# The last 800 steps of a fused attention and MLP kernel in another order, with other engines for some of them

## The chip, the cores and the metric
The kernel runs on one core of one Trainium2 chip. The metric is the device time of one execution in microseconds (us): 209.87 is the median of three runs before (209.62 to 209.92). A profiled run is an execution of its own. Engines are named as in the profile: PE is TensorE's matmuls, PEld its weight loads, DVE is VectorE, ACT is ScalarE, POOL is GpSimd, SP is SyncE, which issues DMAs.

## The reference
Attention over a window of 128 keys and the first 4 keys (sinks), for 4 batches, 8 heads, 768 positions and a head size of 64; its output is the input of an MLP with squared relu, 3072 tokens, 512 to 2048 to 512.

```python
rel = pos[:, None] - pos[None, :]
keep = is_sink | ((rel >= 0) & (rel < window))          # n_sink 4, window 128
scores = np.where(keep, scale * np.matmul(q, k.transpose(0, 1, 3, 2)), -1e9)
a = np.exp(scores - scores.max(-1, keepdims=True))
attn = np.matmul(a / (a.sum(-1, keepdims=True) + 1e-9), v)
x = attn.transpose(0, 2, 1, 3).reshape(B * S, H * D)    # 3072 x 512
r = np.maximum(x @ w_in, 0.0)
out = (r * r) @ w_out
```

## The kernel before
The work is cut into 992 steps, each a small function that issues one or a few instructions. A table, `ORDER`, lists the steps by number in the order in which they are issued. A letter behind a number names the engine of a step that can run on more than one (d DVE, a ACT, g POOL, p PE); without a letter it is the first engine that the step allows. A "+0" or "+1" names the pool of PSUM banks that it takes. `Plan.run` goes through the table from first to last. Every engine works through its own instructions in that order and waits at each for what it needs, so the table sets the queue of each engine, of SP's and POOL's DMA issues too, and the reuse of buffers, which are handed out as they come free in table order: eight `expm` buffers, three `r`, two `osb`, four `sg`, two times two pools of PSUM banks.

The stages of a batch, with the names that the profile shows and the lines that matter here:

- Loads. For batches 2 and 3, q, k and v are loaded by POOL's queue (`qn`, L402, and `v`, L414) and q and k are turned by SP's DMA transposes (`qkT`, L460). For batches 0 and 1 PE turns them (`pt`, L503).
- Scores: PE writes `ps` (L609) and the sinks' scores `pk` (L568); ACT takes exponentials into `expm` (L630) and `es` (L576).
- Masks: the steps `domask` set what lies outside the window to zero. A step with "g" issues two affine selects on POOL (L218), each on 128x512 values; a step with "d" multiplies by a triangle on DVE (L642), 128x1024 values at once. The first of a batch multiplies by `mask0` on DVE (L639).
- Values: PE writes `po` (L678), DVE takes reciprocals (L694) and scales (L695, `xn_sb`); the result is turned into `xT` by PE and a copy (`px`, L727, L192/L194) or by SP's DMA transposes (L709).
- Layer 1 of the MLP: batch 0 as plain products (L762, relu L776 or L778, squares L785 or L787). The other batches use a scheme of seven products for each block of 2x2 (L892) on sums of the inputs (`xs`, L854; `xd` is a spread copy) and of the weights (`wi`, L811). Partial results are kept by a copy `t` (ACT L192 or DVE L194), added and bounded by DVE (`r`, L942), put through a relu (L967 on ACT, L969 on DVE) and squared into `gT_sb` (L915 on ACT, L917 on DVE).
- Layer 2: mostly the same scheme (products `py`, L1239), on four sums of `gT_sb` that DVE makes from 16-bit values (`sg` and in place, L1213, 128x1024 each). Quarters of the output are copied (L192 on ACT, L194 on DVE) or added (L1253, DVE) into `osb`, and SP's queue stores them (L1282). The last tile ends in smaller pieces (L1100 and following).

A copy is issued at L192 when ACT makes it and at L194 when DVE makes it, whatever it copies; the tile's name tells which it is.

Of the kernel before, what the change touches and what calls it, by code (L numbers as in the profile page):

```python
# [21 lines left out]
990 1 0 2 7 8 9 10 11 12 13 14 15 16 17 18 56d 60a 55d 991+0 3 19 57+0 61d 20 5 6 4 62+1 65 59a 67+0 58a 21 64d 89d  # L22
63a 68+0 75+1 88d 69 70 76+1 22 71+0 77 23 72 73 78 24 94a 79+1 90+0 93d 92a 95+1 80 91d 81 96a 74 100+0 82 101+0 25
26 102 83+1 97d 66 84d 27 104 85 110+1 111+0 103g 86d 152+1 112 28 113d 105d 98+0 99 153 106+0 108 114 115d 154a 116+1
118 29 160+1 109 161 162a 107 30 119 117 120+0 31 155d 163a 122 121d 123d 32 168+0 156+1 331 33 172+0 157 169 164+1
170a 165 34 35 158d 173 166a 124+1 125a 127+0 36 159d 176+1 129a 177 126d 174a 140+1 133+1 37 128d 171d 142 136 180+1
181 282+0 38 178d 167d 137d 132+0 141+1 182a 130+0 39 283 40 144 143d 41 134 42 43 332 284 285 131 145d 146+0 175a 147
135g 278 179a 286 138+1 139 287 288 148+0 150 334 151d 44 149a 279 183d 289 184+1 290 185 193+0 280 281 200+0 201 291
194 45 204+1 196+0 202 46 203 205 198a 186 197 207a 293 206 187+0 199a 216+0+0 47 48 195a 217 49 188d 234+1+0 50 235
190+0 219 208+0 87 292 237 209 295 191 218 297+0 189 220 51 336 52 212 53 210a 294 211 255+0 252+1 254 299 298 256 54  # L30
253a 257 444 223+0+1 333 238d 445 192a 226 304 213 224 221+0 312 222 300 241+1+0 301 214+0 296 244 215 302 225 446
303d 242 306 260+0+0 236 462 263 307 314 337 316+0 245d 243d 315 227 308 313 447 318 319 464 246+0 261 247 239+0 448
240 320 321 228+0 475 322d 317 229 258+0 335 259 325 449 450 310 326 230+0 451 231 452 232 248+0 233 249a 327 250 251a
323 309 305 343+1 359+1 339 338 344 467 340 345 341 360 463 329 311 453 324 328 346 465 347 361 362 363 267+1+1 348
349 350 364 268 342 365d 270 351d 366 367 375+0 352 376 377 354 368 454 355 468 356d 370 369a 357 455 391+0 456 379
264 457 262 466 458 265+0 271 393 353 459 378 269 371 392 395 358a 266 372 272+0 373 381 380 382 474 374a 397 394 273
274+0 383d 276 277 396 275a 384 469 407 386 485+0+0 388d 718 472 387 470 460 486 398 410 461 408 389 412+1 488 471
478+1+0 409 399 473 385 479 400 487 330 413 688 402 414 428+0 404 401 403 405 430 416 429 418 432 406a 489 530+0 481
415 390 417 431 419 532 689 526 411 490+0 434 420 433 435 528 421 423 491 436 437 707 482 527 422a 533 424 480 534 690
708 476+0 477 425 439 440 441 691 535 442 531 483+1 426 529 484 443a 536 494+0+0 537 438a 497 692 427 495 568+0 545  # L40
539 540 570 564 566 492 693 694 695 542 498d 501+0+0 502 565 696 541 493 571 504 697 706 538 572 698 543 569 709
517+0+1 518 546 699 573 544 547 520 700 575 503d 510+0+0 701 574 549+0 496d 583 711 576 567 577 584 578 521d 513 505
# [1367 lines left out]
```

## Time and profile before

| | before |
|---|---|
| median of 3 runs | 209.87 us |
| the profiled execution | 209.26 us |
| its span | 207.6 us |
| PE busy | 199.6 us (96%) |
| DVE busy | 174.7 us (84%) |
| ACT busy | 133.9 us (64%) |
| POOL busy | 96.2 us (46%) |

The span runs from the first to the last recorded instruction; 1.66 us of the execution lie around it. Busy times of the engines overlap and don't add up to the span. Times of single rows are in microseconds from the start of the span; a bracket behind a row shows the idle time of the engine before it and who ended it. An instruction on DVE or ACT is shown until its result is written, and the next of the same engine starts a little earlier, so rows of one engine overlap by about 0.1 us.

### The profile page before, as it was taken

The numbers are of one execution on the slowest core, as the hardware profiler recorded it, in microseconds if no ns is written. First come the engines' busy times: TensorE is split into PE (matmuls) and PEld (weight loads), VectorE is DVE, ScalarE is ACT, GpSimd is POOL, SyncE is SP. The second block draws the span as 40 slices with busy tenths as digits, with TensorE's granted clock in tenths as the row PEclk, the third lists the DMA queues.
The fourth block names the chain that finished last, engine by engine and source line by source line (L and its number), as shares of the span: only waits on it lengthen the run. The fifth ranks groups of instructions, "written<-read, shape, count | busy, mean of one in ns | idle before, by whom it ended". The sixth has DMA issues, their size and how long they took to land.

```text
span 207.6 us, 6021 instructions
## 1 busy us (share of the span) xinstructions
PE 199.6 (96%) x2500; PEld 176.2 (85%) x2502; DVE 174.7 (84%) x342; ACT 133.9 (64%) x208; POOL 96.2 (46%) x137
## 2 busy tenths in 40 slices
PE   7969999999899999999999999999999999999993
PEld 7458997579878899889878988998889999999893
DVE  4387657498899998999998778999989998998853
ACT  2769458729998168898888458989871452584010
POOL 7799275699499927999333529000280000000000
PEclk9999999999999999999999999999999999999999
DMA  5999999999999999999999996901023220200205
GB/s 157 220 218 200 186 185 212 180 156 175 159 75 126 147 129 225 117 182 155 123 142 235 103 135 194 115 3 25 12 42 129 53 94 10 104 0 0 104 0 202
DMA packets 96042, 26.10 MB, mean 126 GB/s; under 512 B 86800, under 2 KB 93456, under 8 KB 96016
## 3 DMA queue, kind: packets, MB, share of 16 engines
q0 software_dynamic: 69248, 12.59, 86.5%
q1 hardware_dynamic: 25568, 12.49, 27.2%
q10 hardware_dynamic: 1200, 0.66, 1.1%
q8 instruction: 19, 0.31, 0.6%
q14 instruction: 7, 0.06, 0.1%
HBM read 27.30 MB, written 6.29 MB: 162 GB/s over the span
## 4 chain that ended last, share of the span: by engine, by line
PE 80%; DVE 6%; ACT 6%; DMA 4%; issue 2%; POOL 0%; ACTq 0%; POOLq 0%; DVEq 0%
PE py L1239 28%; PE pm L892 25%; PE pm L762 9%; PE po L678 6%; PE ps L609 4%; DMA v<-in_v_dram 4%; PE py L990 3%; ACT expm L630 2%; PE py L1100 2%; PE pt L503 1%; DVE r L942 1%; ACT gT_sb L915 1%; PE px L727 1%; DVE xn_sb L695 1%; ACT qkT L192 1%
## 5 line engine op out<-in xcount | busy, mean ns | idle before, releaser
L630 ACT ACTIVATE expm<-ps 128x1024 bf16<-128x1024 f32 (+1 forms) x48 | 43.8, 951 | 9.6 <-PE ps L609 7.6
L218 POOL TENSOR_SCALAR_AFFINE_SELECT expm<-expm 128x512 bf16<-128x512 bf16 x34 | 24.0, 740 | 42.2 <-DVE xn_sb L695 19.5
L942 DVE CUSTOM_DVE_ANT_0 r<-pm,t 128x512 bf16<-128x512 f32 x54 | 36.0, 684 | 1.6 <-PE pm L892 1.2
L1239 PEld LDWEIGHTS <-gT_sb 128*128 128x128 bf16 x320 | 30.4, 98 | 4.4 <-issue 0.6
L892 PEld LDWEIGHTS <-w_in_sb 128*128 128x128 bf16 x384 | 32.4, 114 | 1.7 <-issue 1.5
L192 ACT ACTIVATE t<-pm 128x512 f32<-128x512 f32 x42 | 24.7, 600 | 13.4 <-PE pm L892 12.7
L892 PEld LDWEIGHTS <-wi 128*128 128x128 bf16 x288 | 24.7, 114 | 0.8 <-issue 0.7
L1239 PEld LDWEIGHTS <-sg 128*128 128x128 bf16 x240 | 22.5, 98 | 3.1 <-DVE sg L1213 0.3
L192 ACT ACTIVATE osb<-py 128x256 f32<-128x256 f32 (+1 forms) x36 | 14.1, 397 | 15.7 <-PE py L1239 15.0
L762 PE MATMUL pm<-xT,w_in_sb 128*128 128x256 bf16 x192 | 22.5, 273 | 0.1
L892 PE MATMUL pm<-xs,wi 128*128 128x256 bf16 (+1 forms) x192 | 21.6, 246 | 0.0
L892 PE MATMUL pm<-xs,w_in_sb 128*128 128x256 bf16 (+1 forms) x192 | 21.5, 246 | 0.0
L762 PEld LDWEIGHTS <-w_in_sb 128*128 128x128 bf16 x192 | 20.5, 114 | 0.8 <-issue 0.5
L1239 PE MATMUL py<-wt,gT_sb 128*128 128x256 bf16 x160 | 20.7, 273 | 0.2
L1239 PE MATMUL py<-wt,sg 128*128 128x256 bf16 x160 | 20.8, 273 | 0.0
L1239 PE MATMUL py<-w_out_sb,gT_sb 128*128 128x256 bf16 x160 | 20.4, 273 | 0.0
L915 ACT ACTIVATE gT_sb<-r 128x1024 bf16<-128x1024 bf16 x17 | 18.0, 1056 | 1.8 <-DVE r L942 1.6
L678 PE MATMUL po<-v,expm 128*128 128x65 bf16 x352 | 17.9, 193 | 1.1 <-DMA v<-in_v_dram 1.1
L678 PEld LDWEIGHTS <-expm 128*128 128x128 bf16 x352 | 16.8, 97 | 2.3 <-issue 1.3
L695 DVE TENSOR_TENSOR xn_sb<-po,rc 128x512 bf16<-128x512 f32 (+1 forms) x28 | 17.2, 615 | 1.0
L1253 DVE TENSOR_TENSOR osb<-py,osb 128x256 f32<-128x256 f32 x30 | 12.1, 416 | 4.7 <-PE py L1239 4.6
L609 PE MATMUL ps<-qkT 64*128 64x128 bf16 (+1 forms) x256 | 14.5, 238 | 1.1 <-ACT expm L630 0.6
(107 smaller groups left out, 377.8 us busy)
## 6 DMA issues: line engine op xcount, KB each, us to landing
out_dram<-osb SPq DMA_DIRECT2D x11, 512.0 KB, 3.0
v<-in_v_dram POOLq DMA_DIRECT2D x24, 128.0 KB, 7.0
qn<-in_k_dram POOLq DMA_DIRECT2D x20, 128.0 KB, 6.6
qn<-in_q_dram POOLq DMA_DIRECT2D x20, 128.0 KB, 6.3
w_in_sb<-in_moe_w_in_dram POOLq DMA_DIRECT2D x4, 512.0 KB, 9.2
w_out_sb<-in_moe_w_out_dram POOLq DMA_DIRECT2D x4, 512.0 KB, 10.5
qr<-in_k_dram SPq DMA_DIRECT2D x4, 256.0 KB, 6.9
qr<-in_q_dram ACTq DMA_DIRECT2D x2, 256.0 KB, 4.2
```

Of the source, the lines that this page charges most:

```text
L192: return nc.scalar.activation(out=dst, in_=src, func=AF.Copy)
L218: nc.gpsimd.affine_select(out=e_tile, in_=e_tile, compare_op=ALU.is_ge, fill=fill, base=i - 1, pattern=[[0, n], [1 if i else -1, 128]], ch ...
L609: nc.tensor.matmul(ps[:, h2, o:o + w], lhsT=qkT_sb[r, m, 1, c, :], rhs=qkT_sb[r, m, 0, qb:qb + w // 128, :], start=(i == 0 and not biased) ...
L630: nc.scalar.activation(out=x[:, :, o:512], in_=bank_t["s", b, s, m][:, :, o:512], func=AF.Exp, scale=scale)
L678: touch(("po", b, s, m0), e, nc.tensor.matmul(pv[:, i, h2, :], lhsT=lhsT, rhs=rhs, start=(n_ == 0), stop=(n_ == len(mms) - 1)), j)
L695: touch(("po", b, s, m0), e, nc.vector.tensor_tensor(out=xn_sb[:, 2 * s:2 * s + 2, 128 * (m0 + j0):128 * (m0 + j0 + nj)].rearrange("p i (j ...
L762: nc.tensor.matmul(pm[:, i, :], lhsT=w_in_sb[:, fb // 4, kb, fb % 4:512:4], rhs=xT[:, c0 // 256:(c0 + cw) // 256, kb, :], start=(kb == 0), ...
L892: touch(tag, e, nc.tensor.matmul(y[:, bk, i, :], lhsT=weights(name, f0 + i, a), rhs=rhs[:, a, :], start=fresh and i == 0 and a == 0, stop= ...
L915: nc.scalar.activation(out=d, in_=x, func=AF.Square)
L942: touch(tag, e, nc.vector._custom_dve(TENSOR_ADD_SAT, out=d.rearrange("p n c -> p (n c)"), in0=T["y"][:, 1].rearrange("p n c -> p (n c)"), ...
L1239: touch((b, u), e, nc.tensor.matmul(region(name), lhsT=x[:, i, :], rhs=w_[:, i, :], start=first and i == 0, stop=i == HB - 1, skip_group_c ...
L1253: ins = nc.vector.tensor_tensor(out=d, in0=region(of), in1=d, op=ALU.add)
```

## The change
Only the table changes. Its first 188 words keep their steps and engines (to about 49 us of the span); the remaining some 800 stand in another order, and every step that has a choice now has its letter written out. The table is four lines longer, so every line behind it has a number greater by 4 (L218 is L222, L630 L634, L642 L646, L915 L919, L917 L921, L1213 L1217, L1239 L1243, L1253 L1257). The number of steps and the matmuls are the same. GpSimd keeps 17 mask steps and DVE 27, but three change sides each way (238, 512 and 749 go to POOL; 236, 519 and 765 to DVE). Among the steps whose engine changes: of the squares of layer 1 eleven go from DVE to ACT and three back; of the copies `t` six go to ACT and four back; of the output quarters six and three.

The lines of the table where it begins to differ, and its end:

```diff
 ...
-135g 278 179a 286 138+1 139 287 288 148+0 150 334 151d 44 149a 279 183d 289 184+1 290 185 193+0 280 281 200+0 201 291
 ...
-953 971 947 952 958 975 949 959d 956 972 960 950 961 973 977+0 962 976 978 964 954 966 979d 965 963 980 968 981 982
-985 967d 969 983 984 989 986 988 987
 ...
+151d 44g 149a 279d 183d 289 290a 293d 184+1 196+0 45g 200+1 291a 185a 204+1 197 199a 205 46g 212g 201 193+1 186a 280d
 ...
+974+1 971d 948a 975 952d 957a 953d 958 972d 959a 954d 956 977+1 960 949d 961a 944d 973d 950 962 964d 976a 980d 965 966
+978 967a 968d 981 979a 982 963d 985 969 983d 984d 989 986d 988 987d
 ...
```

Three places show what moves. The first is DVE in layer 2 of batch 2, at the sums L1213, before (the row `L694` is the reciprocal of the values of batch 3):

```order
L917 TENSOR_TENSOR gT_sb<-r 128x2x2x256
L942 ISA r<-pm,t 128x512
L1253 TENSOR_TENSOR osb<-py,osb 128x256
L1213 TENSOR_TENSOR sg<-gT_sb 128x1024
L1213 TENSOR_TENSOR gT_sb<-gT_sb 128x8x128
L1213 TENSOR_TENSOR sg<-sg,gT_sb 128x1024
L694 RECIPROCAL rc<-po 128x8
L695 TENSOR_TENSOR xn_sb<-po,rc 128x2x2x128
```
And with the change:

```order
L946 ISA r<-pm,t 128x512
L921 TENSOR_TENSOR gT_sb<-r 128x2x2x256
L1217 TENSOR_TENSOR sg<-gT_sb 128x1024
L1257 TENSOR_TENSOR osb<-py,osb 128x256
L1217 TENSOR_TENSOR gT_sb<-gT_sb 128x8x128
L1217 TENSOR_TENSOR sg<-sg,gT_sb 128x1024
L646 TENSOR_TENSOR expm<-expm,tri 128x1024
L1257 TENSOR_TENSOR osb<-py,osb 128x256 x2
L198 COPY osb<-py 128x256
```
A quarter stands between the first two sums, and a mask of batch 3 (step 765, `expm` times `tri`), which POOL did before, follows the three sums on DVE.

The second place is ACT in layer 1 of batch 1, from the spread copy `xd` on, before:

```order
L192 ACTIVATE xd<-xT_185 128x1024
L630 ACTIVATE expm<-ps 128x2x384 x2
L192 ACTIVATE t<-pm 128x512
L630 ACTIVATE expm<-ps 128x2x384
L192 ACTIVATE t<-pm 128x512
L967 ACTIVATE r<-pm 128x512
L192 ACTIVATE t<-pm 128x512 x2
L915 ACTIVATE gT_sb<-r 128x2x2x256
L630 ACTIVATE expm<-ps 128x2x384
L192 ACTIVATE osb<-py 128x256
L192 ACTIVATE t<-pm 128x512 x3
```
And with the change:

```order
L196 ACTIVATE xd<-xT_185 128x1024
L634 ACTIVATE expm<-ps 128x2x384 x2
L196 ACTIVATE t<-pm 128x512 x2
L634 ACTIVATE expm<-ps 128x2x384
L971 ACTIVATE r<-pm 128x512
L919 ACTIVATE gT_sb<-r 128x2x2x256
L196 ACTIVATE t<-pm 128x512 x2
L634 ACTIVATE expm<-ps 128x2x384
L919 ACTIVATE gT_sb<-r 128x2x2x256
L196 ACTIVATE t<-pm 128x512 x2
L196 ACTIVATE osb<-py 128x256
```
A second square (step 401) stands behind the relu, and the quarter `osb` (step 532) has gone behind the last two copies `t`.

The third place is POOL at the masks of the last batches, its loads of batch 3 among them, before:

```order
L402 DMA qn<-in_k_dram 128x8x64 x2
L218 AFFINE_SELECT expm<-expm 128x4x128 x6
L402 DMA qn<-in_q_dram 128x8x64 x2
L218 AFFINE_SELECT expm<-expm 128x4x128 x6
L414 DMA v_182<-in_v_dram 128x8x64 x2
L218 AFFINE_SELECT expm<-expm 128x4x128 x8
```
And with the change:

```order
L406 DMA qn<-in_k_dram 128x8x64
L222 AFFINE_SELECT expm<-expm 128x4x128 x2
L406 DMA qn<-in_k_dram 128x8x64
L222 AFFINE_SELECT expm<-expm 128x4x128 x4
L406 DMA qn<-in_q_dram 128x8x64 x2
L222 AFFINE_SELECT expm<-expm 128x4x128 x8
L418 DMA v_182<-in_v_dram 128x8x64 x2
L222 AFFINE_SELECT expm<-expm 128x4x128 x6
```
Of the two key loads one has gone behind the first two selects, and the loads of v behind two more.

More of the change, by code (lines that the diff above doesn't have):

```diff
@@ L57 @@
[L57 to L58 removed]
+990d 1d 0d 2d 7 8a 9 10a 11 12 13 14 15 16 17 18 56d 60a 55d 991+0 3g 19g 57+0 61d 20g 5g 6g 4g 62+1 65g 59a 67+0 58a
+21g 64d 89d 63a 68+0 75+1 88d 69a 70a 76+1 22g 71+0 77a 23g 72d 73 78a 24g 94a 79+1 90+0 93d 92a 95+1 80d 91d 81 96a
+74d 100+0 82d 101+0 25g 26g 102a 83+1 97d 66a 84d 27g 104a 85 110+1 111+0 103g 86d 152+1 112a 28g 113d 105d 98+0 99a
```

69 lines of the change are left out of this document (35 added, 34 removed).

## The prediction
> **What bounds the kernel now.** I read the chain of work that ended last, then busy time by stretches of the span, then the waits of TensorE (PE and its weight loads, PEld), and last the timeline at each of those waits.
>
> ```profile
> PE 80%; DVE 6%; ACT 6%; DMA 4%; issue 2%; POOL 0%; ACTq 0%; POOLq 0%; DVEq 0%
> ```
> The chain lies on PE for 80% of the span. The stretches say where (length, then busy time of PE, PEld, DVE, ACT, POOL, the granted clock, and DMA):
>
> ```profile
> 0.00:20.00 20.00, 16.37 (x219) 12.79 (x220) 11.62 (x33) 13.16 (x20) 16.07 (x31) 1.00 1.24 199
> 49.00:75.00 26.00, 25.40 (x337) 21.98 (x335) 24.44 (x49) 18.94 (x33) 21.91 (x30) 1.00 2.15 136
> 75.00:110.00 35.00, 34.85 (x459) 31.19 (x458) 34.00 (x64) 31.03 (x48) 23.10 (x31) 1.00 1.97 156
> 128.00:155.00 27.00, 26.87 (x348) 24.29 (x347) 25.50 (x47) 23.96 (x37) 7.05 (x10) 1.00 0.34 63
> 204.00:207.60 3.60, 0.21 (x4) 0.04 (x1) 0.54 (x3) 0.00 (x0) 0.00 (x0) 0.97 0.55 194
> ```
> PE idles 3.63 us before 20 us and 3.39 us after 204. The new order is the same up to about 49 us, and its last products and three last stores stand in the same order, so neither end moves. What the change can win lies between: little, because PE is busy nearly throughout there, while DVE (34.00 of 35) and ACT (31.03 of 35) run close behind it from 75 to 110 us. There, PE, DVE and ACT are all near their limit at once. The clock was granted at 1.00.
>
> Busy PE may still be spread out. The waits that the profile names for PE and PEld from 49 to 204 us (total, times, longest) are these:
>
> ```profile
> PE ps L609 <- ACT expm L630: 0.6, 1, 0.6
> PE pm L892 <- ACT expm L630: 0.2, 1, 0.2
> PEld L609 <- issue: 3.8, 16, 0.7
> PEld L1239 <- DVE gT_sb L1213: 0.4, 1, 0.4
> PEld L1239 <- DVE sg L1213: 0.3, 1, 0.3
> PEld L1239 <- DVE osb L194: 0.2, 1, 0.2
> ```
> Of the weight loads' "issue" waits at the scores (L609), fifteen of sixteen come to about 0.2 us each ((3.8 - 0.7) / 15); they stand at the switch into 64-row score groups. Both orders have 20 such switches after the common part, so I price them at no change. What the order can touch is the named waits, about 1.7 us together, and a few unnamed tenths.
>
> **The change part by part.** Its parts are: PE's steps change neighbours; eleven squares of the MLP go from DVE to ACT and three back; of the layer-1 copies `t` six go to ACT and four come back, of the quarters of the output six and three, and a handful of others change by ones; three pairs of masks change sides between GpSimd and DVE, their number staying 17 steps; POOL's loads stand elsewhere among the masks.
>
> *Waits that go.* The rows are from the timeline (start, length, and in brackets the idle time before and who ended it):
>
> ```profile
> 61.32 0.77 PEld L1239 LDWEIGHTS <-sg 128*128 128x128 bf16 x8
> 62.94 0.55 PEld L1239 LDWEIGHTS <-sg 128*128 128x128 bf16 x6 [0.16 <-DVE osb L194]
> 71.83 0.99 PEld L1239 LDWEIGHTS <-gT_sb 128*128 128x128 bf16 x8
> 153.66 2.22 PE L1239 MATMUL py<-wt,gT_sb 128*128 128x256 bf16 x16
> 155.71 0.49 PE L1239 MATMUL py<-w_out_sb,gT_sb 128*128 128x256 bf16 x3
> 192.45 1.04 PE L1239 MATMUL py<-wt,gT_sb 128*128 128x256 bf16 x8
> 193.52 1.05 PE L1239 MATMUL py<-wt,sg 128*128 128x256 bf16 x8
> 194.40 0.82 PE L1100 MATMUL py<-wt,gT_sb 128*128 128x256 bf16 x6
> ```
> An undisturbed product step of eight matmuls starts 0.88 us before the next (193.52 to 194.40). At 62.94 PE waits 0.16 for a copy of a quarter (L194); in the new order scores and a product change places there and the copy has more time: 0.16 saved. At 71.83 eight loads take 0.99, 0.22 more than the eight at 61.32; that product (step 327) moves later: 0.2. At 153.66 two steps take 2.05 start to start in place of 1.76: 0.29, the price of a sum on DVE that came late. At 192.45 a step takes 1.07: 0.19; in the new order other products stand ahead of this one. Together 0.84. Three smaller gaps between 125 and 142 us, each a tenth or so, I put at 0.2 of gain from a bound of 0 to 0.3. Sum: **1.04 us** saved.
>
> *Why the sum at 153.7 was late.* DVE and POOL at that place:
>
> ```profile
> 153.59 1.67 POOL L218 TENSOR_SCALAR_AFFINE_SELECT expm<-expm 128x512 bf16<-128x512 bf16 x2 [0.48 <-ACT expm L630]
> 153.69 1.07 DVE L1213 TENSOR_TENSOR gT_sb<-gT_sb 128x1024 bf16<-128x1024 bf16 x1
> 107.19 0.68 DVE L1213 TENSOR_TENSOR gT_sb<-gT_sb 128x1024 bf16<-128x1024 bf16 x1
> 81.80 0.69 DVE L917 TENSOR_TENSOR gT_sb<-r 128x1024 bf16<-128x1024 bf16 x1
> 81.28 1.69 POOL L218 TENSOR_SCALAR_AFFINE_SELECT expm<-expm 128x512 bf16<-128x512 bf16 x2
> ```
> The same 16-bit sum takes 0.68 us (107.19) and 1.07 us beside a GpSimd mask (153.69): 0.39 more. At 81.28 it is the pair of masks that is longer, while the DVE step in it (81.80) keeps its 0.69. So the one that starts second waits. The new order puts the mask of this place on DVE, behind the sums: the stretch goes, and 0.29 of PE's time with it. The mask now costs DVE about 0.68, which lies under PE's products after that, since DVE had 1.5 us free in this stretch (25.50 of 27). Without that cover it would cost up to 0.68.
> The Trainium skill, "SBUF — State Buffer", section "Who interferes with whom", says that a VectorE instruction with both inputs in SBUF shares a read interface with GpSimd, that whoever issues first holds it whole, and that issue order decides. The rows here agree (0.68 against 1.07). By that rule a list that fixes the order on each engine does not fix who is first of two engines; it stands behind the first rival below.
>
> *Engine moves.* Net, eight squares, two copies `t` and three quarters leave DVE for ACT; their prices are in the groups (busy time, mean ns of one):
>
> ```profile
> L915 ACT ACTIVATE gT_sb<-r 128x1024 bf16<-128x1024 bf16 x17 | 18.0, 1056 | 1.8 <-DVE r L942 1.6
> L917 DVE TENSOR_TENSOR gT_sb<-r 128x1024 bf16<-128x1024 bf16 x19 | 13.3, 701 | 0.4
> L192 ACT ACTIVATE t<-pm 128x512 f32<-128x512 f32 x42 | 24.7, 600 | 13.4 <-PE pm L892 12.7
> L194 DVE COPY t<-pm 128x512 f32<-128x512 f32 x12 | 8.2, 685 | 1.0 <-ACT expm L630 0.6 <-PE pm L892 0.4
> L1253 DVE TENSOR_TENSOR osb<-py,osb 128x256 f32<-128x256 f32 x30 | 12.1, 416 | 4.7 <-PE py L1239 4.6
> ```
> DVE loses 8 x 0.70 + 2 x 0.69 + 3 x 0.42 = 8.2 us of work; ACT gains 8 x 1.06 + 2 x 0.60 + 3 x 0.4 = 10.9 us. Neither is on PE's path as a total: PE idles 0.15 us from 75 to 110 us, so DVE's relief can pay no more than that there beyond the waits already counted.
> The Trainium skill, "Perfetto Trace Analysis", section "Optimizing Scalar/DVE Operations", says that offloading a saturated VectorE to ScalarE may make sense. If DVE's 8.2 us set the end, the sum would be near 201 us; the rows above, with PE busy for 34.85 of 35, allow no such thing, and the trace speaks against it here.
>
> *A new wait.* Where ACT is dense, the added squares push other work back. Between a spread copy of batch 1's input (`xd`) and a product that needs a later copy `t`, ACT did this among other work:
>
> ```profile
> 87.19 1.06 ACT L192 ACTIVATE xd<-xT 128x1024 bf16<-128x1024 bf16 x1 [0.40 <-DVE xT L194]
> 92.91 1.05 ACT L915 ACTIVATE gT_sb<-r 128x1024 bf16<-128x1024 bf16 x1
> 93.86 0.80 ACT L630 ACTIVATE expm<-ps 128x768 bf16<-128x768 f32 x1
> 94.55 0.39 ACT L192 ACTIVATE osb<-py 128x256 f32<-128x256 f32 x1
> 94.81 1.10 ACT L192 ACTIVATE t<-pm 128x512 f32<-128x512 f32 x2
> 96.13 0.61 PE L892 MATMUL pm<-xd,wi 128*128 128x128 bf16 x8
> ```
> Its second `t` ends at 94.81 + 1.10 = 95.91, and the product that reads it starts at 96.13: 0.22 us of room. The new order has one square more between (0.95 us start to start, 92.91 to 93.86) and one quarter less (0.26, 94.55 to 94.81): 0.69 more, so the copy comes 0.47 late. Queued behind it on PE is a product of layer 2, and all later products. I take **0.4 us** (between 0, if ACT's own idle pieces shrink, and 0.69). The wait at 52.6 us (0.58, for ACT's exponential) stands among the same rows in both orders and stays.
>
> *Loads.* POOL, in its own order:
>
> ```profile
> 99.13 1.78 POOL L402 DMA_DIRECT2D qn<-in_k_dram  x2 [0.24 <-DMA v<-in_v_dram]
> 107.23 2.17 POOL L218 TENSOR_SCALAR_AFFINE_SELECT expm<-expm 128x512 bf16<-128x512 bf16 x2 [6.32 <-issue]
> 115.07 1.78 POOL L402 DMA_DIRECT2D qn<-in_q_dram  x2
> ```
> One key load of batch 3 is put behind two masks, so from about 100 us to about 110 us. It is still 5 us ahead of the query loads (115.07) that the same scores need, so it costs nothing. The last two v loads go behind two further masks and so some 1.3 us later, or by as much as their exponentials take; SP's transposes and stores keep their order but for neighbours. Bound: 0 to 0.9, one load's time on POOL; I take 0, as no PE wait above names a DMA.
>
> The sum: 209.26 (the profiled run; its span is 207.60, with 1.66 around it) - 1.04 + 0.4 = 208.62. The median of the three runs is 209.87, 0.61 above the profiled run, so the forecast is **209.2 us**.
>
> **The rivals.**
> *First: nothing to see.* The masks start when ACT's exponential ends, which no list fixes: the mask at 153.59 had waited 0.48 for it. If as many stretches fall on other sums (0.39 each), the two late sums return (0.48) and only 0.16 + 0.2 stay, less the 0.4 on ACT: 209.87 - 0.36 + 0.4 = **209.9**. For it: POOL is busy 21.91 of 26 and 23.10 of 35 where DVE is densest. Against it: the swap of the mask at 153 removes its neighbour entirely.
> *Second, slower: ACT becomes the bound from 75 to 110 us.* It is busy 31.03 of 35 now. Two of the squares that move stand in that stretch, 0.95 each, and copies with them. From the point where ACT's room of 0.22 us at the product of 96.13 is gone, each further square is paid in full: 1.9 us, less 1.04 saved elsewhere: 209.87 + 0.86 = **210.7**. For it: the sum above is already past that point by 0.47. Against it: other work is taken from ACT in the same stretch, and it had pieces of idle time (13.4 us before its `t` copies over the whole run, nearly all in waiting for PE).
> *Third: more is won.* If the ACT wait is absorbed and PE's 0.31 us at 89 us goes as well:
>
> ```profile
> 89.00 0.45 PEld L892 LDWEIGHTS <-w_in_sb 128*128 128x128 bf16 x7 [0.31 <-issue]
> ```
> then 209.87 - 1.04 - 0.31 = **208.5**; with the 0.58 at 52.6 too, 207.9, the least that the waits allow.
>
> **How the numbers follow.** Forecast 0.43, more won 0.12, nothing to see 0.27, slower 0.18. A measurement of this kernel can tell about 0.2%, 0.42 us, from no change: faster means below 209.45, slower above 210.29. So faster 0.55, same 0.27, slower 0.18. The forecast's own range is 208.7 to 209.6. The range reaches from 208.1 to 210.5: the lower end leaves out only the far part of the third case, and the upper end only the far part of the second, under 2 in 10 together.
>
> **What would show it.** Right: no wait of PEld for `gT_sb` or `sg` behind the sums (L1213, four lines further down now) between 150 and 195 us; a DVE busy time near 166 us and ACT near 144; a PE wait of 0.3 to 0.5 us for ACT's `t` near 95 us. Wrong: as many DVE sums over 1 us as before (first rival); ACT over 33 of 35 from 75 to 110 us, with several PE waits for it (second); a wait of PE for `qkT` behind a DMA, which I price at nothing.

## The result, and the profile after

| | before | changed |
|---|---|---|
| median of 20 runs each, us | 209.91 | 212.41 |
| lowest to highest, us | 209.03 to 210.53 | 209.67 to 216.75 |
| ratio, 95% interval | | 1.0068 (1.0039 to 1.0096) |
| profiled execution, us | 209.26 | 209.67 |
| its span, us | 207.6 | 208.0 |

The changed kernel is slower by 0.7%, 1.4 us, where 209.2 us and a gain of 0.3% were forecast; the predicted range (208.1 to 210.5) does not hold the median. Its runs lie 7 us apart, those of before 1.5 us. The ratio leaves out executions more than 1.5% above the fastest of the same kernel (8 of the 20 here), so it is smaller than that of the two medians, and where a trace below is of such a longer execution its time is given.

The profiled execution was one of the fastest (209.67), so this page shows what the change gains and what it costs at best. The share of the chain of work that ended last, by engine (before, PE had 80%, DMA 4%):

```profile
PE 73%; DMA 18%; POOL 3%; DVE 2%; ACT 1%; issue 1%; ACTq 0%; DVEq 0%; POOLq 0%
```

DMA stands for 18% of it, all ahead of 47.8 us: this one chain runs back through the single wait for a load that is shown below, so the 18% is not a cost. The stretches that answer to those of before (length, then busy time of PE, PEld, DVE, ACT, POOL, clock, DMA), and the first of them in the kernel before:

```profile
20.00:49.00 29.00, 28.45 (x324) 23.73 (x323) 20.39 (x38) 17.25 (x22) 19.18 (x25) 1.00 1.74 191
49.00:75.00 26.00, 25.42 (x334) 22.20 (x333) 23.97 (x46) 18.32 (x31) 24.13 (x31) 1.00 1.91 131
75.00:110.00 35.00, 34.59 (x455) 30.77 (x454) 32.73 (x60) 31.98 (x51) 20.33 (x29) 1.00 1.84 143
128.00:155.00 27.00, 27.00 (x356) 24.54 (x355) 25.76 (x48) 24.94 (x39) 4.31 (x6) 1.00 0.37 70
```
```profile
20.00:49.00 29.00, 28.89 (x327) 24.35 (x326) 20.46 (x37) 16.84 (x21) 19.04 (x25) 1.00 1.83 181
```

PE wins 0.13 us from 128 to 155 us, and loses 0.44 from 20 to 49 and 0.26 from 75 to 110. Of the named waits of PE and PEld from 20 to 204 us, the largest that are new:

```profile
PE pt L507 <- DMA qn<-in_q_dram: 0.4, 1, 0.4
PE po L682 <- DVE r L946: 0.3, 1, 0.3
...
PEld L507 <- DMA qn<-in_q_dram: 0.6, 1, 0.6
PEld L682 <- POOL expm L222: 0.5, 1, 0.5
```

These are two places. The first is PE's turns of batch 1's q, behind a load on POOL's queue; PE of the changed kernel, the piece of its chain of work that names the load, and PE of before:

```profile
46.30 1.00 PE L507 MATMUL pt<-ident,qn 128*128 128x128 bf16 x15
47.75 0.68 PE L507 MATMUL pt<-ident,qn 128*128 128x128 bf16 x9 [0.45 <-DMA qn<-in_q_dram]
```
```profile
40.48 7.22 DMA qn<-in_q_dram
```
```profile
48.13 1.06 PE L503 MATMUL pt<-ident,qn 128*128 128x128 bf16 x16
```

The turns start at 46.30 in place of 48.13, because a layer-1 product (step 193) now stands behind the first of them; the load lands at 40.48 + 7.22 = 47.70, in time for the old place and too late for the new. The second place is values of batch 1 (DVE, POOL, PE):

```profile
79.56 1.08 DVE L921 TENSOR_TENSOR gT_sb<-r 128x1024 bf16<-128x1024 bf16 x1
```
```profile
79.47 2.92 POOL L222 TENSOR_SCALAR_AFFINE_SELECT expm<-expm 128x512 bf16<-128x512 bf16 x4 [5.04 <-ACT expm L634]
```
```profile
81.13 0.60 PE L896 MATMUL pm<-xT,wi 128*128 128x256 bf16 x4
81.56 0.60 PE L896 MATMUL pm<-xT,w_in_sb 128*128 128x256 bf16 x4
82.49 0.22 PE L682 MATMUL po<-v,expm 128*128 128x65 bf16 x2 [0.32 <-DVE r L946]
```

A square (step 353) now stands on DVE ahead of the addition (357) that frees the bank for these values. Beside four selects it takes 1.08 us in place of 0.70 (the mean of the squares on DVE before), and the values start 0.50 us late: four matmuls pass in 0.43 (81.13 to 81.56), so they were due at 81.99 and start at 82.49. At the sums where a gain was forecast, DVE shows what was forecast:

```profile
153.04 0.68 DVE L1217 TENSOR_TENSOR gT_sb<-gT_sb 128x1024 bf16<-128x1024 bf16 x1
153.64 0.68 DVE L1217 TENSOR_TENSOR sg<-sg,gT_sb 128x1024 bf16<-128x1024 bf16 x1
```

Both sums take 0.68; the 1.07 of before is gone. So in one of the shortest executions gains and losses nearly meet. What ordinary executions of the changed kernel show beyond that is in the next section.

### The profile page after: what moved, and what is told of

The parts are those of the page before. It is cut to its first block, busy times and chain, and to the rows that moved or that the text cites. A ratio compares the mean times of both kernels' runs of the same rounds, so it can differ in the third digit from the quotient of the medians.

```text
span 208.0 us, 6028 instructions
## 1 busy us (share of the span) xinstructions
PE 198.8 (96%) x2500; PEld 175.7 (84%) x2502; DVE 168.0 (81%) x329; ACT 142.7 (69%) x221; POOL 95.6 (46%) x137
## 4 chain that ended last, share of the span: by engine, by line
PE 73%; DMA 18%; POOL 3%; DVE 2%; ACT 1%; issue 1%; ACTq 0%; DVEq 0%; POOLq 0%
PE py L1243 30%; PE pm L896 27%; DMA w_out_sb<-in_moe_w_out_dram 6%; DMA qn<-in_k_dram 6%; PE po L682 5%; PE ps L613 4%; DMA qn<-in_q_dram 3%; DMA qr<-in_q_dram 3%; PE pm L766 3%; PE py L1104 2%; POOL w_in_sb L311 1%; PE pt L507 1%; POOL v L384 1%; POOL vs L554 1%; PE px L731 1%
## 5 line engine op out<-in xcount | busy, mean ns | idle before, releaser
L634 ACT ACTIVATE expm<-ps 128x1024 bf16<-128x1024 f32 (+1 forms) x48 | 43.8, 953 | 6.0 <-PE ps L613 5.4
L222 POOL TENSOR_SCALAR_AFFINE_SELECT expm<-expm 128x512 bf16<-128x512 bf16 x34 | 23.3, 724 | 44.3 <-ACT expm L634 36.4
L1243 PEld LDWEIGHTS <-gT_sb 128*128 128x128 bf16 x320 | 30.3, 98 | 4.3 <-issue 0.7
L196 ACT ACTIVATE t<-pm 128x512 f32<-128x512 f32 x44 | 25.6, 606 | 9.5 <-PE pm L896 8.6
L196 ACT ACTIVATE osb<-py 128x256 f32<-128x256 f32 (+1 forms) x39 | 15.0, 399 | 20.6 <-PE py L1243 19.8
L919 ACT ACTIVATE gT_sb<-r 128x1024 bf16<-128x1024 bf16 x25 | 26.2, 1060 | 1.3 <-DVE r L946 1.3
L1243 PEld LDWEIGHTS <-sg 128*128 128x128 bf16 x240 | 22.5, 98 | 3.3 <-issue 0.6
L896 PE MATMUL pm<-xs,w_in_sb 128*128 128x256 bf16 (+1 forms) x192 | 21.0, 246 | 0.0
L1243 PE MATMUL py<-wt,sg 128*128 128x256 bf16 x160 | 20.8, 273 | 0.0
L1243 PE MATMUL py<-wt,gT_sb 128*128 128x256 bf16 x160 | 20.6, 273 | 0.0
L1243 PE MATMUL py<-w_out_sb,gT_sb 128*128 128x256 bf16 x160 | 20.3, 273 | 0.0
L1257 DVE TENSOR_TENSOR osb<-py,osb 128x256 f32<-128x256 f32 x30 | 12.0, 418 | 5.8 <-PE py L1243 2.7
```

The source lines that it names most:

```text
L196: return nc.scalar.activation(out=dst, in_=src, func=AF.Copy)
L222: nc.gpsimd.affine_select(out=e_tile, in_=e_tile, compare_op=ALU.is_ge, fill=fill, base=i - 1, pattern=[[0, n], [1 if i else -1, 128]], ch ...
L634: nc.scalar.activation(out=x[:, :, o:512], in_=bank_t["s", b, s, m][:, :, o:512], func=AF.Exp, scale=scale)
L896: touch(tag, e, nc.tensor.matmul(y[:, bk, i, :], lhsT=weights(name, f0 + i, a), rhs=rhs[:, a, :], start=fresh and i == 0 and a == 0, stop= ...
L919: nc.scalar.activation(out=d, in_=x, func=AF.Square)
L1243: touch((b, u), e, nc.tensor.matmul(region(name), lhsT=x[:, i, :], rhs=w_[:, i, :], start=first and i == 0, stop=i == HB - 1, skip_group_c ...
```

## The experiments

Three theories were set against each other. **Late transfers**: the new order puts loads and DMA transposes later on POOL's and SP's queues, or their readers earlier on PE, so that PE now waits for them. **Engines**: the forecast gains do not exist, or ACT and DVE lose more than they gain. **Looseness**: any other order of these queues is as much slower, with runs as far apart. In the short diffs below, words of the table are steps; a line without a sign is context. Every kernel was timed against the kernel before on the same chip.

### The changed kernel again

No edit. 

> The changed kernel once more, unedited, for the spread of its times and a second trace. In its first trace PE waited 0.62 us at 47 us for a q load of batch 1, and two DMA transposes (steps 464 and 716) were issued only 4.8 and 3.0 us ahead of the scores that need them. Theory A (PE waits for transfers that now land just in time): times between 209.7 and 217 again, and a trace of a longer run has longer waits of PE at one or more of these three places, and nowhere else. Rival B (TensorE's clock): the longer runs show a lower granted clock and no longer wait. Rival C (the engines, ACT or the masks): the waits that differ between the two traces end with ACT, DVE or POOL.

Measured: 214.08 us (210.99 to 215.11, 6 runs), ratio 1.0151 (1.0101 to 1.0202). That does not overlap with the first interval: the ratio of a kernel whose runs lie so far apart is less certain than its interval says, and differences of half a per cent between such kernels settle nothing below. Its profiled execution took 214.11 us, span 212.4. Waits of PE and PEld, and PE's timeline there:

```profile
PE ps L613 <- DMA qkT<-qn: 2.4, 1, 2.4
```
```profile
PEld L613 <- DMA qkT<-qn: 2.7, 1, 2.7
```
```profile
90.89 0.50 PE L613 MATMUL ps<-qkT 64*128 64x256 bf16 x8 [2.44 <-DMA qkT<-qn]
```

These are the first scores of batch 2 (step 485), which read a q transpose (464). On SP, before and in this execution:

```profile
60.73 12.71 SPq L460 DMA_TRANSPOSE qkT<-qn  x4
```
```profile
73.15 19.01 SPq L464 DMA_TRANSPOSE qkT<-qn  x8
```

In the order of before 464 is among the four from 60.73 on; in the new one it is the fifth of the eight from 73.15 on, behind 466, 468, 469 and 472, each of which reads a load of its own. The lateness feeds on itself, since POOL's loads wait for transposes to free `qn`:

```profile
93.43 1.76 POOL L406 DMA_DIRECT2D qn<-in_k_dram  x2 [4.91 <-DMA qkT<-qn]
```

And the stall has an echo in PE's granted clock (the column behind POOL's busy time):

```profile
92.00:93.00 1.00, 1.00 (x9) 0.82 (x8) 1.00 (x2) 0.78 (x2) 0.00 (x0) 0.68 1.09 208
93.00:94.00 1.00, 1.00 (x11) 0.80 (x11) 0.61 (x3) 0.60 (x1) 0.57 (x1) 0.50 0.69 262
94.00:95.00 1.00, 1.00 (x11) 0.57 (x11) 1.00 (x3) 0.95 (x2) 1.00 (x2) 0.50 0.64 262
95.00:96.00 1.00, 1.00 (x11) 0.82 (x10) 0.36 (x1) 0.57 (x2) 1.00 (x2) 0.61 1.40 90
```

The clock lost in these four rows is 0.32 + 0.50 + 0.50 + 0.39 = 1.71 us, so it was at half for some 3.4 us (1.71 / 0.50). Stall and echo together are 2.44 + 1.71 = 4.15 of the 4.4 us by which this span is longer than the other one of the same kernel.

### Are the transfers' places enough?

Into the kernel before went only the new places of the loads and transposes of batches 2 and 3 and of the copies of two sink keys (475, 719); all else stays (e_dma_new). The piece that the scores of batch 2 hang on:

```diff
-464 246+0 261 247
+246+0 261 247
...
-391+0 456 379
+391+0 468 469 472 464 473 379
```

> The kernel before with only the loads and DMA transposes of batches 2 and 3 at their new places, and the two copies of sink keys that need them; PE, DVE and the squares as before. Theory A: the waits of PE for qkT appear (up to 2.7 us at the scores of batch 2 and up to 3.2 us at the sink scores of batch 3) and the times spread from 210 to 216. Rival B: times stay at 209.0 to 210.6.

Measured: 212.95 us (210.86 to 216.22, 7 runs), 1.0088 (1.005 to 1.0127). Waits of PE, and the stretch from 75 to 110 us:

```profile
PE ps L609 <- DMA qkT<-qn: 2.2, 1, 2.2
```
```profile
75.00:110.00 35.00, 32.52 (x417) 29.01 (x415) 31.16 (x60) 28.73 (x46) 21.14 (x30) 0.95 1.82 149
```

The same wait at the same scores, the same fall of the clock, and a loss as large as the whole change's (1.0068), though but for the two copies the order of every engine's own work is that of before. The places of the transfers are enough for such a loss; the theory of the engines is not needed for it.

The reverse, the changed kernel with those transfers at the places of before (e_dma_old):

```diff
-391+0 468 469
+391+0
...
+462 464
```

> The changed kernel with the loads and DMA transposes of batches 2 and 3 put back at the places that they had before the change (by the progress of PE's steps; SP's queue of transposes in the old order), everything else as changed. Theory A (the transfers' new places are what spreads the times): no wait of PE for qkT behind a DMA at the scores of batch 2 or the sink scores of batch 3; the wait for the q load of batch 1 at 47 us stays (0 to 1.8 us); times 209 to 211. Rival B (PE's and the engines' new order reaches those steps too early, whatever the queues' order): waits for qkT stay and the times spread up to 216.

Measured: 210.87 us (209.75 to 216.21, 12 runs), 1.0037 (1.0018 to 1.0056). The ratio is lower than the first, but by less than the half per cent that settles nothing, and the runs still reach 216. Its profiled execution took 213.48 us. PE still waits there for a q transpose, at the sink scores of batch 3 (`pk`), although it stands at its old place; the second row is the last of these transposes on SP's queue:

```profile
PE pk L572 <- DMA qkT<-qn: 2.4, 1, 2.4
```
```profile
129.19 1.20 SPq L464 DMA_TRANSPOSE qkT<-qn  x1
```

The queue is done with it at 129.19 + 1.20 = 130.39, and PE starts `pk` at 133.68, 3.3 us later. In the first trace of the changed kernel the queue was done with its last one at 125.59 + 2.50 = 128.09, and `pk` started at 129.88, 1.8 us later, without a wait. So the old places by themselves do not keep this transfer in time beside the changed order of the engines, and the time from the queue to the landing differs between these two executions by over 1 us.

### One late transfer at a time

All of these are edits of the changed kernel. Transpose 464 back behind 462 (e_464):

```diff
-462
+462 464
...
-393d 464 473
+393d 473
```

> The changed kernel with one DMA transpose of batch 2's q (step 464) put back right behind the first of them on SP's queue, at about 68 us where it stood at 83. If its late landing ahead of the scores at 87.7 us makes the times spread, they lie within 1.5 us of each other, near 209.7; if the q load at 47 us or the clock does, they spread up to 217 as in the changed kernel. The fast end stays at 209.7 either way.

Measured: 212.35 us (209.68 to 216.23, 12 runs), 1.0083 (1.0049 to 1.0116). Waits of PE, and two stretches:

```profile
PE pt L507 <- DMA qn<-in_q_dram: 1.8, 2, 1.5
PE pk L572 <- DMA qkT<-qn: 1.5, 1, 1.5
```
```profile
49.00:75.00 26.00, 23.91 (x317) 20.82 (x316) 22.69 (x43) 17.34 (x29) 24.00 (x31) 1.00 2.02 114
...
128.00:155.00 27.00, 25.49 (x337) 22.97 (x335) 24.49 (x45) 23.83 (x37) 5.88 (x9) 1.00 0.38 73
```

The wait at the scores of batch 2 is gone, and the kernel is no faster: in this execution PE waits 1.5 us for a q load (turns of batch 1, 49 to 75) and 1.5 for a q transpose (sink scores of batch 3, `pk`, 128 to 155). There is not one late transfer but at least three, and each is late in some traces and not in others.

Product 193 back ahead of batch 1's q turns (e_q193), and both edits (e_both):

```diff
-204+1 197 199a 205 46g 212g 201 193+1
+193+0 204+0 197 199a 205 46g 212g 201
```

> The changed kernel with step 193 (1.75 us of batch 0's layer 1 on PE) put back ahead of the turns of batch 1's q, so that these need the load about 1.7 us later, as before the change. If the q load is what costs, the wait of 0.62 us at 47 us is gone and the fastest runs come to 209.1; if it is also what makes the times spread, they lie within 1.5 us of each other like those of the kernel before. If the spread comes from the later transposes or from the clock, the times spread up to 217 as in the changed kernel, 0.6 us lower at the fast end.

> Both edits together. If the two transfers are the whole loss, the times come to about 209.1, within 1.5 us of each other, faster than the kernel before by 0.3 to 0.4%. If there is a third place (the transpose step 716 ahead of 129.9 us, or the clock), they still spread by over 2 us.

Measured: 214.75 us (211.94 to 216.46, 6 runs), 1.0124 (1.0088 to 1.016), and 212.84 us (211.49 to 214.75, 6 runs), 1.0129 (1.0094 to 1.0164). The wait for the q load is gone from both traces, and neither helps. In the trace of e_both PE waits 2.6 us for the q transpose at `pk`, and 1.3 us at a layer-1 product, for the bank that 193 now takes: an effect of my own edit. The same edit with the relu of 193 (step 194) moved too, on top of e_dma_old (e_fix), fell to the same kind of wait, 2.1 us for a relu on ACT, and to 2.9 at `pk`.

> As the first of these three, and also with step 193 ahead of the turns of batch 1's q, its relu ahead of the turns' copies on ACT so that the next step of layer 1 takes its PSUM bank (in the run e_q193 that step waited 1.3 us for a copy on DVE). If the three transfers are the whole loss: no wait of PE behind a DMA after 45 us, all times within 1.5 us of each other, and 209.1 to 209.5, since the mask that PE waits 0.49 us for at 82 us stays. If something else spreads the times, they reach over 212.

Measured: 214.07 us (213.23 to 215.64, 6 runs), 1.0217 (1.0177 to 1.0257). It did not do what was expected.

SP alone: 464 behind 462, and 708, 713 and 712 ahead of the store 544 (e_sp).

```diff
-544 550 511a 701g 708
+708 713 712 544 550 511a 701g
```

> The changed kernel with two edits on SP's queue alone: step 464 right behind the first transpose of batch 2, and three transposes of batch 3 (708, 713, 712) ahead of the store of batch 1's first tile (544), which waits for DVE until about 109 us while they could already run. Theory A, sharpened: SP passes one transpose in 1.25 us, and 13 of them behind that store end at 128.1, too late for the sink scores at 129.9; three fewer end 3 us earlier. So no wait of PE for qkT at either place; the waits for batch 1's q loads (47 and 57 us) stay, and the times spread from 209.5 to some 213. Rival: the transposes take longer than before wherever they stand, and waits for qkT stay.

Measured: 211.75 us (210.95 to 213.5, 6 runs), 1.0102 (1.0059 to 1.0144). No wait for a transpose is left in its trace, and its runs reach to 213.5 only; PE still waits 1.0 us at a turn of batch 1 for a q load.

Next 464 behind 462 with the loads 702 and 703 ahead of the masks 512 and 514 (e_two), then also 193 and 194 behind 185 (e_three), then also the square 353 behind the addition 357 (e_best). (The diff shows the loads and the square.)

```diff
-507d 581d 580a 514g 500d 702g 552 713 522+0 719a 703g
+702g 703g 507d 581d 580a 514g 500d 552 713 522+0 719a
...
-366 353d 466
+366 466
...
-357d 378d
+357d 353d 378d
```

> The changed kernel with step 464 right behind the first DMA transpose of batch 2 on SP's queue, and the last two q loads of batch 3 (steps 702 and 703) ahead of the four affine selects on POOL's queue that they stood behind (POOL was idle for 3.2 us there, waiting for an exponential). Theory A: no wait of PE for qkT at the scores of batch 2 nor at the sink scores of batch 3; the wait for batch 1's q load at 47 us stays, 0 to 2 us, and with it a spread from 209.7 to some 212. Rival: if waits for qkT stay, it isn't the place in the queues but the time that the transfers take.

> The same, and step 193 (1.75 us of PE) with its relu put ahead of the turns of batch 1's q, on a PSUM bank that the next step of layer 1 gets back in time. Theory A: all three waits are gone, the times lie within 1.5 us of each other at 209.0 to 209.7. If a fourth place spreads the times, they reach over 212 with a wait at another line.

> The same, and on DVE the 16-bit square that took 1.08 us beside GpSimd's masks at 79.6 us (step 353) put behind the two additions (L946) that follow it, the second of which frees the PSUM bank that the values at 82 us wait for. If that stretch is what makes PE wait 0.49 us there, that wait goes and the time falls by 0.4 to 0.5 us against the run before it, to 208.6 to 209.2. If the wait is for the masks themselves, as one row of the profile says, nothing changes.

Measured: e_two 212.54 us (209.65 to 217.5, 12 runs), 1.0047 (1.0021 to 1.0074); e_three 210.65 us (209.36 to 217.03, 12 runs), 1.0015 (0.9985 to 1.0044); e_best 213.11 us (210.47 to 215.25, 10 runs), 1.0115 (1.0075 to 1.0154). In the trace of e_two, of its execution of 215.96 us, PE still waits 2.8 us at `pk`, although the loads stand earlier, and 2.0 us for q loads. With three groups of transfers and their readers moved, the interval of e_three includes no change, though its runs still reach to 217. Waits of PE in its trace:

```profile
PE pk L572 <- DMA qkT<-qn: 0.9, 1, 0.9
...
PE po L682 <- DVE r L946: 0.3, 1, 0.3
```

e_best is slower again. The values of batch 1 in its trace (PE), and POOL and DVE there:

```profile
82.08 0.23 PE L682 MATMUL po<-v,expm 128*128 128x65 bf16 x2
```
```profile
81.24 1.22 POOL L222 TENSOR_SCALAR_AFFINE_SELECT expm<-expm 128x512 bf16<-128x512 bf16 x2 [0.48 <-ACT expm L634]
```
```profile
81.90 1.10 DVE L921 TENSOR_TENSOR gT_sb<-r 128x1024 bf16<-128x1024 bf16 x1
```
```profile
85.45 0.22 PE L682 MATMUL po<-v,expm 128*128 128x65 bf16 x2 [0.93 <-DVE xn_sb L699]
```

The first values now start at 82.08, as soon as the products ahead of them allow, although the second pair of selects ends only at 82.46. So in the changed kernel it was DVE's addition behind the square that held them, and not the selects, which the row of PEld names. But behind the addition the square meets the second pair, is again stretched to 1.10, and now holds up the norm `xn_sb`: the next values, in the last row, wait 0.93 in place of 0.50.

All edits of transfers at once, step 212 behind 52 and 193 ahead of the turns (e_fix2):

> The changed kernel with all transfers mended: the two edits on SP's queue, the last q loads of batch 3 ahead of the four selects, the step that fills vs for batch 1 (212, 3.2 us on POOL) behind batch 1's q loads as before the change, and step 193 ahead of all turns of batch 1 on the PSUM banks of the kernel before. Theory A: no wait of PE behind a DMA after 20 us; all times within 1.7 us of each other; 209.0 to 209.5, that is 0.1 to 0.4% faster than the kernel before, since the wait of 0.49 us at 82 us stays. If a further place waits, the times still spread beyond 212.

Measured: 212.9 us (210.33 to 215.3, 6 runs), 1.0104 (1.0048 to 1.0159). In its longest run, the profiled one, a fourth place shows: 3.9 us at a layer-2 product for an `osb` buffer, which store 544 holds, and I had put that store late. Nothing more is concluded from it.

### Is it the turns?

Into the kernel before, only 193 and 194 behind the turn 197 (e_qearly):

```diff
-185 193+0 280 281 200+0 201 291 194 45 204+1 196+0 202 46 203 205 198a 186 197
+185 280 281 200+1 201 291 45 204+1 196+0 202 46 203 205 198a 186 197 193+1 194
```

> The kernel before with step 193 and its relu behind the turns of batch 1's q, as in the changed kernel: that part of the change alone. Theory A: PE waits up to 2 us for the q load at 47 us in some runs and the times spread from 209.5 to some 212. If that wait is harmless, the times stay at 209.0 to 210.6.

Measured: 211.81 us (211.42 to 212.28, 6 runs), 1.0093 (1.0066 to 1.0119). Waits of PE:

```profile
PE ps L609 <- ACT expm L630: 0.9, 1, 0.9
PE pt L503 <- DMA qn<-in_q_dram: 0.7, 1, 0.7
```

It has the wait for the load (0.7) and, since the order of ACT around it is still that of before, others of its own. So it shows that the load is just in time there, and no price for this piece alone.

### Where in the program is the loss?

The order of before up to step 720, at 129 us, then the changed one (e_late):

> The order of the kernel before up to and with step 720 (the sink scores of batch 3, at 129 us), then all that is left in the order and on the engines of the changed kernel. All loads and transposes ahead of that point stand as before the change. Theory A: no wait behind a DMA, times within 1.7 us of each other; of the gains in the changed kernel only those after 129 us are left (the sum at 153.7 us, 0.30, and some 0.1 of small gaps): 0.3 to 0.4 us under the kernel before, ratio 0.998 to 0.999. If the spread comes from the late part, the times reach 212 and more.

Measured: 209.66 us (209.14 to 210.67, 12 runs), 1.0007 (0.9986 to 1.0029). Neither a loss nor long runs: both come from the order ahead of 129 us. Nor a gain, though the wait at 153.7 is gone from its trace. In the span from 75 to 110 us it is the kernel before:

```profile
75.00:110.00 35.00, 34.85 (x459) 31.26 (x458) 33.99 (x65) 30.93 (x48) 23.09 (x31) 1.00 2.11 155
```

The first 253 words of before, then the changed order with 464 and 708 early, 353 on ACT and 358 on DVE (e_hyb):

> The order of the kernel before up to batch 1's last turns (57 us), so that batch 1's q loads are needed as late as they were, then the changed order; on SP's queue steps 464 and 708 as early as before; and to end the wait at 82 us the square of step 353 on ACT and that of step 358 on DVE instead. Theory A: no wait behind a DMA; the gains at 61, 72, 88, 154 us (0.15, 0.19, 0.31, 0.30) less 0.15 on ACT are left: 0.6 to 0.9 us under the kernel before, ratio 0.996 to 0.997. If the transposes of batch 3 still land late (13 of them less one behind the store at 109 us), the times spread beyond 212.

Measured: 211.65 us (210.65 to 216.39, 10 runs), 1.009 (1.006 to 1.012). No wait for a transfer is in its trace, but 0.8 us at values of batch 1 for DVE's norm, and it is slower all the same. Ahead of that norm DVE had waited 0.80 us (at 84.06) for one of two squares on ACT, where the edit had put 353, so this wait may be of my own making. That late transfers are not all of the loss is likely from this run; that the order of DVE and ACT is the rest is not shown by it.

### Are the forecast gains real?

Three of the change's small edits in the kernel before, no transfer moved (e_small): scores 260 behind product 316, product 327 behind bridge 250, mask 765 on DVE.

```diff
-306 260+0+0 236 462 263 307 314 337 316+0 245d
+306 236 462 307 314 337 316+0 260+0+0 261 263 245d
...
-249a 327 250 251a
+249a 250 327 251a
...
-763 782 765
+763 782 765d
```

> The kernel before with three of the change's small edits and nothing else: the scores 260 (with 261 and 263) stand behind product 316, the product 327 stands behind bridge 250, and mask 765 is on VectorE. No load, transpose or store moves. Theory (the waits that the change removes are real gains, and only the moved transfers turn them into a loss): the waits of 0.15, 0.19 and 0.30 us go, 0.64 us in all, so about 209.0 against 209.6 to 209.8 of the kernel before, ratio about 0.997, and its runs as close together as the kernel before's (1.5 to 2 us from lowest to highest). Rival (the waits come back elsewhere, or TensorE's queue takes them up): ratio 1.000 with as close runs. Second rival (any other order of VectorE's and TensorE's work is as loose as the changed kernel): ratio 1.005 or more with runs 5 us apart.

Measured: 211.51 us (210.71 to 211.91, 6 runs), 1.0071 (1.0054 to 1.0088). Slower. Waits of PE, and PE's timeline at the place:

```profile
PE py L1239 <- ACT osb L192: 1.1, 1, 1.1
...
PE py L1239 <- DVE osb L194: 0.5, 1, 0.5
```
```profile
62.62 1.05 PE L1239 MATMUL py<-wt,sg 128*128 128x256 bf16 x8
64.19 1.03 PE L1239 MATMUL py<-w_out_sb,sg 128*128 128x256 bf16 x8 [0.51 <-DVE osb L194]
```

With the scores gone from between them, products of layer 2 follow one another faster than copies of the quarters free `py`'s banks: 1.6 us for a gain of 0.15. The scores there were the spacer that hid the copy. The next kernel leaves the edit at 260 out (e_small2), and its time bears this out. In another, product 190 was also put ahead of scores 234, at PE's largest wait of before (e_small3):

```diff
-249a 327 250 251a
+249a 250 327 251a
...
-763 782 765
+763 782 765d
...
-188d 234+1+0 50 235 190+0 219
+188d 190+0 234+1+0 50 235 219
```

(The last pair is e_small3 alone.)

> The kernel before with two of the change's small edits: product 327 behind bridge 250, and mask 765 on VectorE. The scores 260 stay where they were, because in the run before this one product 316 ahead of them made three products follow one another, and TensorE waited 1.1 and 0.5 us for the bank of `py`. Theory (the forecast gains are real where nothing else moves): 0.19 and 0.29 us go, 0.48 in all, ratio 0.998 with runs 1.5 to 2 us apart. Rival (a wait that goes is found again in the next room that is short): 1.000. Second rival (any edit of the order makes it looser): 1.003 or more.

> e_small2, and layer-1 product 190 ahead of the scores 234, at TensorE's largest wait behind 20 us in the kernel before (0.58 us at 52.6 for ACT's exponential), which the change leaves as it is. Theory: the 0.58 goes too, so 1.06 us in all, ratio 0.995. Rival (190 wants a bank of `pm` that is not yet free, or its evacuation comes ahead of an exponential that is then late): the wait changes its name, ratio 0.998 to 1.000. Slower than 1.002 would say that the place of one product costs more than a wait that the trace names.

Measured: e_small2 208.99 us (208.65 to 210.04, 12 runs), 0.9967 (0.9948 to 0.9985), faster than the kernel before and the changed one; e_small3 210.19 us (209.84 to 211.4, 12 runs), 1.0028 (1.0006 to 1.005). In e_small2's trace PE is busy throughout from 128 to 155 us, where it had idled 0.13 (stretch), though DVE's first sum is still long there, 1.01 us beside the selects that stayed on POOL (DVE):

```profile
128.00:155.00 27.00, 27.00 (x358) 24.71 (x356) 25.33 (x47) 23.74 (x38) 6.43 (x9) 1.00 0.34 65
```
```profile
153.44 1.01 DVE L1213 TENSOR_TENSOR sg<-gT_sb 128x1024 bf16<-128x1024 bf16 x1 [0.83 <-ACT gT_sb L915]
```

PE's two products there take 1.75 us from start to start (154.45 to 156.20) where they took 2.05: the mask's 0.3 us. Of the other edit the trace shows no gain. PE around product 327:

```profile
71.19 1.06 PE L727 MATMUL px<-ident,xn_sb 128*128 128x128 bf16 x16
72.29 1.03 PE L1239 MATMUL py<-wt,gT_sb 128*128 128x256 bf16 x8
```

From the product ahead of these rows to layer 1 behind them PE takes 3.72 us (70.31 to 74.03), and before it took 3.71 (70.33 to 74.04): PEld still idles 0.17 us at the product's weights. This trace is also of one of its longer executions (209.74 us), with a new wait of 0.6 us for an exponential at values near 114 us.

In e_small3 the 0.58 us that PE waited at 52.6 is gone, and a larger wait follows (PE, then ACT):

```profile
55.83 0.38 PE L503 MATMUL pt<-ident,qn 128*128 128x128 bf16 x4 [1.60 <-ACT expm L630]
```
```profile
54.05 2.64 ACT L630 ACTIVATE expm<-ps 128x1024 bf16<-128x1024 f32 x3 [1.49 <-PE ps L609]
```

The scores come later by the product, ACT sits idle for 1.49 us, and the three exponentials that follow hold up the turns: 1.60 lost for 0.58 won. The wait was ACT's working time, not PE's bad luck.

## Why the prediction was wrong

- **The step that failed** is the paragraph on loads: that SP's transposes and stores keep their order "but for neighbours", that the loads cost nothing, "as no PE wait above names a DMA", with a bound of 0.9. A trace without a wait for a DMA says that every transfer was in time; it does not say by how much. I worked out the room of ACT's copies to 0.22 us and did not ask for the room of one transpose (the time from its landing to the start of its reader), though I had the order of SP's queue before me. Step 464 went from the 2nd to the 9th of batch 2's twelve transposes, which is no change of neighbours. In its place the runs show 0.9% for the places of the transfers by themselves (1.0088, 1.0050 to 1.0127), some 1.8 us. They also show that the old places are not enough beside the new order of the engines (2.4 us at `pk` in one execution of e_dma_old): what counts is a transfer's place against its reader's. The sentence on what would show it wrong, a wait of PE for `qkT` behind a DMA, "which I price at nothing", names what was seen, but no rival carried it.
- **"The same up to about 49 us"** failed too. PE's turns of batch 1 differ from 46.3 us on, and cost 0.45 us in the profiled execution.
- **The gains were right in kind.** The waits at 71.8 and 153.7 are gone from the changed kernel's trace, also the 0.31 at 89 that I left to the third rival. e_small2, with two of these edits, gains 0.33% (0.15 to 0.52%) for the 0.23% that they were worth by the sum; but its trace shows only the 0.3 us at 153.7, 0.14%, and nothing at 71.8. So that the sum fits is in part luck, and the 0.2 at 71.8, which I read from the length of weight loads, is not confirmed by moving product 327 alone. One of these gains by itself can be too small to see (e_late). The wait at 192.45 did not go: PEld's wait for the last sum stays 0.3 us long.
- **The rule on the shared interface** was right where I used it (1.07 became 0.68), and I took it for one place only. The first rival said that as many stretches may fall elsewhere; one does, at the square of 79.56, with 0.50 us of PE. Moving that square frees the values that it held and holds the next ones longer (e_best), so the cause is seen, and a better place was not found.
- **The wait on ACT** near 95 us (0.4) did not come: no wait of PE for ACT's `t` is in the trace, though ACT is busy 31.98 of 35. The second rival, ACT as the bound, is not what made it slower, although its time, 210.7 us, is the nearest of all to the measured ratio's: that is chance.
- **The spread** was not in the prediction at all. At the same scores PE waited 0 us in one execution of the changed kernel and 2.44 in another. An explanation that fits this, and the 1.5 us of e_late and of the kernel before, is that a transfer whose reader comes just in time turns differences in how long it takes into differences at the end. It was only argued.

What stays open: which share of the loss each late transfer has (after one is mended, another appears, and intervals of such loose kernels are too unsure); why e_sp and e_hyb, with no transpose late in their traces, are still 1% slower, beyond the waits that these single traces show (that of e_sp is of its shortest run); and why the same transfer takes longer in one execution than in another, which wasn't tried.

## What to carry to other kernels

A transfer for which no profile names a wait may still have next to no room. Before a step is moved past transfers on a DMA-issuing queue, or their reader is moved ahead, take the landing time and the reader's start from several traces, and price what is left against how much that transfer varies. Move one thing at a time: of a change of 800 steps two small edits were worth 0.33% together, and by the ratios the rest of it lost some 1% (1.0068 / 0.9967). An instruction that looks like an interruption between two products may be what hides the copy that frees their bank.

## What the runs showed of the hardware

**A stall of PE can halve its clock afterwards, or not.** After waits of 2.44 us (the changed kernel again) and 2.18 (e_dma_new) the granted clock fell, to 0.50 in the rows above, and the echo cost 1.7 us, nearly as much as the stall. It also fell after 2.1 us (e_fix), 2.8 (e_two), 3.2 (e_q193, in 216.08 us) and 3.9 (e_fix2, in 215.3 us), and in all six traces the lost clock adds up to the same 1.7 us, however long the stall was. After 2.6 us in e_both it did not fall; its stretch with that wait:

```profile
128.00:155.00 27.00, 24.42 (x327) 22.03 (x325) 23.46 (x44) 22.85 (x35) 5.58 (x9) 1.00 0.40 75
```

It did not fall either after 2.9 us (e_fix, at `pk`), 2.4 (e_dma_old), 1.6 (e_small3) and 1.5 (e_464). So between 2.1 and 2.9 us the length of the stall does not decide. The Trainium skill, "TensorE: Matmul & The Clock Gate", section "What's actually happening", has the clock at half after an idle window of about 3.4 us, and says that the window runs freely and does not start with the work. The clock of 0.50 and its length of about 3.4 us agree; but all the stalls here except that of 3.9 us are shorter than such a window, and five of them were enough. That it depends on where in a window the stall falls would explain why 2.6 us cost nothing and 2.18 did; no run here shows the window itself.

One such fall takes 1.7 of some 212 us, which leaves a mean clock of 0.992. Of the 20 runs of the changed kernel seven have that or less, but the run of 214.18 us has 0.999: falls of the clock lengthen the long runs and are not needed for them.
